# One written-out program order exchanged for another in a single-core RWKV-7 plus wave-mixer kernel

## The chip, the cores and the metric

One core of one Trainium2 chip. The metric is the device time of one launch in microseconds. Five engines work from queues of their own, each strictly in its program order: TensorE (PE), VectorE (DVE), ScalarE (ACT), GpSimd (POOL), and SyncE (SP), which here only issues transfers.

## The reference

The reference runs a state recurrence over 768 steps for 4 batches and 8 heads of width 40, and feeds its result, laid out as 4 x 768 x 320, to a mixer:

```python
for t in range(S):
    y[:, :, t] = np.einsum('bhd,bhde->bhe', rt, state)
    Sa = np.einsum('bhde,bhe->bhd', state, at)
    state_decay = state * wt[:, :, None, :] - np.einsum('bhd,bhe->bhde', Sa, bt)
    state = state_decay + np.einsum('bhd,bhe->bhde', vt, kt)
...
theta = x @ w_theta
zr, zi = x * np.cos(theta), x * np.sin(theta)
yr = np.einsum('ts,bsd->btd', w_tok_r, zr)
yi = np.einsum('ts,bsd->btd', w_tok_i, zi)
u = x + yr + yi
return u + np.maximum(u @ w_ch, 0.0)
```

## The kernel before

The 768 steps of a batch are cut into 6 chunks of 128; with 4 batches there are 24 chunks, numbered 0 to 23. The kernel first builds a list of 1610 operations (`plan.add`), each with an engine, a kind and a chunk number, and then emits them in an order that is written out by hand in the constant `ORDER`. Within an engine that order is the queue's order. `HOMES` gives the PSUM bank of each PSUM tile in the order in which they are opened, `PICK` lists the operations that take their second engine (a copy on DVE instead of ACT, a product on DVE instead of POOL, a mask on ACT followed by a select on POOL), and `WARM` puts dummy matmuls (L953) before a few early PE operations. No scheduler decides anything after that.

The names that the prediction uses, always with the chunk number behind them:

- SP loads (L408, L420): `lw`, `la`, `lk`, `lb`, `lv` bring one chunk of one input, 160 KB in pieces of 160 bytes; `loadr` brings half of a pair of chunks of `r` in pieces of 1280 bytes. Each load waits for the load eight places before it, and `st` stores a finished row block (L854).
- POOL: `kb` (L428, two of them per chunk, one from `lk` and one from `lb`) and `ah` (L428, from `la`) are products; `r` (L434) and `v` are casts; `wgt` (L650) is the new state; `z` (L811) are the mixer's products; `sel` (L568) is the select that completes a mask which was begun on ACT; `wdma` (L866, L894) starts a weight's transfer from POOL's queue.
- PE: `tkb`, `ta`, `tr` (L390, L524) are the transposes of `kb`, `ah`, `r`; `spsi`, `sphi`, `slv`, `slu` (L555) are score products, which use the array in two halves of 64 rows; `nu` (L614) needs the masked `phi` of its chunk; `gd` (L390) is the transpose of the state that `wgt` wrote; `wt` (L902) is the transpose of a mixer weight that `wdma` brought; `row` (L827) is the mixer's sum over tokens; `th` and `ch` (L711, L721) are the two dense products of the mixer.
- DVE: the four masks (L564, 1.2 us each), copies out of PSUM (L396) and small sums.

The recurrence runs from chunk to chunk; the loads and the preparation run one to four chunks ahead of it. The mixer's rows for one batch stand between the operations of the next batch, and those of the last batch at the end.

The emission itself is a plain loop:

```python
for o in plan.order():
    if o.idx in WARM:
        ...
    if o.fn is not None:
        o.fn()
```

Of the kernel before, what the change touches and what calls it, by code (L numbers as in the profile page):

```python
# [24 lines left out]
    0, 7, 3, 6, 1, 20, 2, 21, 23, 24, 32, 27, 8, 30, 22, 4, 33, 31, 9, 34, 25, 5, 26, 12, 28,  # L25
    11, 69, 35, 36, 10, 29, 70, 37, 47, 44, 40, 48, 72, 45, 38, 41, 18, 71, 49, 73, 39, 46, 98,
    19, 119, 99, 58, 14, 42, 100, 120, 57, 76, 15, 101, 122, 50, 121, 13, 123, 75, 74, 79, 106,
    102, 53, 107, 51, 131, 108, 16, 77, 125, 80, 52, 78, 109, 132, 126, 43, 81, 134, 124, 103,
    110, 133, 111, 82, 17, 84, 137, 104, 56, 138, 129, 112, 83, 85, 87, 130, 127, 54, 88, 156,
    128, 86, 59, 55, 157, 146, 89, 184, 143, 90, 147, 105, 158, 139, 60, 61, 159, 187, 97, 135,  # L30
    62, 164, 144, 188, 148, 160, 165, 96, 191, 140, 136, 161, 93, 166, 145, 141, 185, 167, 213,
    186, 194, 214, 149, 189, 142, 91, 162, 168, 150, 215, 163, 169, 190, 216, 92, 195, 221,
    234, 170, 151, 192, 152, 222, 246, 235, 193, 237, 217, 236, 95, 238, 202, 218, 94, 196,
    241, 203, 63, 197, 247, 155, 171, 239, 248, 219, 199, 172, 220, 198, 223, 249, 240, 200,
    271, 64, 267, 244, 272, 242, 299, 245, 205, 201, 273, 243, 224, 300, 173, 301, 154, 261,
    274, 254, 302, 174, 262, 225, 303, 279, 206, 175, 258, 306, 176, 255, 153, 259, 280, 263,
    250, 177, 204, 281, 256, 212, 275, 496, 282, 260, 211, 226, 251, 257, 305, 252, 320, 264,
    276, 253, 283, 317, 349, 227, 327, 265, 277, 328, 497, 304, 309, 278, 208, 329, 498, 284,
    310, 266, 499, 330, 207, 350, 285, 307, 351, 318, 286, 270, 308, 354, 331, 352, 500, 311,
    268, 332, 287, 361, 319, 314, 353, 312, 336, 269, 333, 539, 362, 337, 289, 356, 363, 209,  # L40
    315, 288, 313, 290, 364, 338, 355, 387, 210, 291, 339, 540, 292, 316, 365, 116, 388, 322,
    357, 366, 113, 541, 389, 359, 358, 340, 390, 501, 360, 367, 325, 334, 542, 503, 391, 368,
    382, 373, 392, 376, 412, 502, 374, 506, 369, 411, 504, 321, 377, 375, 393, 416, 507, 524,
    505, 370, 181, 394, 378, 525, 326, 508, 418, 335, 371, 526, 341, 372, 323, 415, 509, 395,
    396, 527, 413, 528, 342, 510, 514, 178, 511, 397, 517, 117, 529, 595, 545, 398, 512, 118,
    384, 530, 572, 399, 544, 532, 531, 573, 596, 515, 400, 513, 533, 574, 554, 597, 383, 401,
    543, 402, 417, 379, 575, 598, 516, 534, 385, 403, 380, 114, 599, 546, 581, 115, 548, 582,
    414, 535, 576, 381, 549, 550, 583, 404, 601, 555, 551, 577, 642, 536, 182, 324, 584, 557,
    578, 427, 179, 556, 567, 66, 558, 180, 183, 585, 561, 386, 428, 559, 537, 600, 586, 568,
    419, 602, 538, 560, 604, 587, 522, 429, 547, 605, 420, 606, 619, 421, 552, 607, 626, 562,  # L50
    553, 434, 423, 627, 564, 435, 422, 436, 565, 563, 643, 518, 628, 425, 437, 644, 610, 629,
    519, 566, 424, 613, 645, 603, 588, 611, 630, 520, 426, 589, 438, 698, 430, 635, 231, 646,
    523, 631, 612, 439, 636, 431, 632, 745, 440, 571, 608, 432, 614, 609, 699, 647, 521, 746,
    700, 675, 747, 648, 637, 570, 433, 615, 676, 616, 701, 633, 293, 677, 748, 651, 634, 678,
    638, 649, 590, 652, 684, 579, 569, 296, 685, 679, 617, 580, 639, 706, 653, 228, 591, 654,
    592, 657, 686, 680, 593, 618, 620, 661, 594, 687, 650, 441, 702, 711, 703, 621, 640, 442,
    712, 655, 662, 688, 681, 658, 656, 689, 705, 659, 622, 641, 682, 663, 660, 664, 690, 704,
    667, 749, 665, 691, 683, 709, 68, 692, 707, 710, 67, 729, 668, 666, 708, 694, 65, 693, 695,
    730, 750, 719, 697, 713, 720, 670, 696, 731, 232, 732, 294, 672, 233, 297, 714, 721, 295,
    733, 298, 738, 229, 751, 739, 734, 716, 715, 230, 740, 624, 717, 735, 754, 450, 752, 451,  # L60
    755, 778, 718, 452, 346, 625, 741, 779, 453, 881, 756, 343, 780, 623, 454, 757, 408, 781,
    882, 742, 764, 883, 405, 767, 765, 782, 884, 669, 673, 444, 783, 455, 443, 768, 456, 671,
    445, 766, 784, 446, 736, 885, 457, 785, 737, 458, 760, 743, 459, 753, 448, 786, 787, 887,
    722, 744, 796, 761, 788, 769, 758, 460, 763, 759, 789, 762, 461, 790, 462, 888, 797, 912,
    792, 463, 791, 447, 913, 793, 770, 795, 892, 771, 794, 914, 893, 723, 915, 772, 886, 674,
    802, 773, 890, 464, 803, 891, 347, 905, 465, 916, 348, 344, 799, 917, 805, 409, 345, 406,
    920, 804, 407, 896, 811, 726, 466, 921, 473, 897, 410, 474, 725, 808, 475, 918, 467, 809,
    724, 898, 468, 922, 469, 899, 927, 798, 449, 476, 471, 919, 477, 889, 906, 900, 801, 928,
    478, 929, 960, 470, 807, 480, 728, 930, 961, 901, 481, 482, 923, 806, 962, 955, 483, 963,
    894, 935, 484, 931, 479, 800, 969, 924, 895, 485, 970, 940, 983, 932, 486, 964, 727, 941,  # L70
    902, 965, 1030, 971, 934, 908, 903, 925, 972, 1031, 907, 819, 933, 820, 1032, 926, 904,
    487, 776, 810, 821, 1033, 488, 822, 984, 966, 775, 936, 985, 938, 1035, 937, 986, 823, 774,
    824, 939, 1086, 489, 825, 973, 490, 987, 777, 491, 1034, 949, 494, 946, 942, 812, 492, 813,
    950, 1087, 1037, 814, 1088, 1007, 974, 1036, 1089, 943, 951, 957, 975, 815, 990, 945, 816,
    947, 817, 493, 944, 1041, 989, 1039, 956, 1042, 818, 976, 948, 1040, 1014, 988, 958, 977,
    826, 1015, 952, 991, 827, 472, 1052, 953, 1090, 1016, 909, 967, 1017, 994, 992, 968, 995,
    1053, 979, 954, 993, 978, 1018, 1133, 996, 911, 1019, 1054, 980, 997, 998, 981, 1001, 1020,
    910, 999, 982, 828, 1023, 1002, 1092, 1058, 1134, 829, 1024, 959, 1000, 830, 1135, 1091,
    1004, 1049, 1005, 1136, 835, 1008, 1093, 836, 833, 1095, 831, 1009, 1063, 1003, 1050, 1096,
    837, 838, 1010, 1064, 1097, 1038, 1006, 1021, 1098, 1051, 1065, 1110, 1022, 1025, 1066,  # L80
    1104, 1026, 1045, 1043, 1072, 1044, 839, 1105, 840, 1067, 1073, 1027, 1011, 1046, 1068,
    1269, 1074, 841, 1047, 1069, 1012, 1270, 1075, 1028, 1048, 1094, 1013, 1271, 1117, 1138,
    1099, 1029, 1061, 1118, 1076, 1055, 1100, 1272, 1101, 1139, 1060, 1137, 1119, 1056, 1077,
    1120, 1059, 1140, 1070, 1126, 1071, 1142, 1102, 1057, 1127, 1161, 1106, 1144, 1143, 1121,
    1128, 1315, 1122, 1103, 1107, 1145, 1078, 865, 1123, 1108, 866, 1129, 867, 1111, 1141,
    1316, 1166, 1148, 1317, 1124, 1112, 1130, 1167, 1318, 1155, 1125, 1152, 1273, 1156, 1062,
    1146, 1168, 1276, 1149, 1169, 1113, 868, 1147, 1153, 1157, 869, 1275, 1150, 1131, 1115,
    1151, 1079, 1274, 1132, 1154, 870, 495, 1080, 1170, 1293, 871, 1280, 1319, 1109, 1278,
    1171, 1281, 1371, 1158, 1279, 1172, 1320, 1159, 1300, 1173, 1081, 1372, 1114, 1321, 1082,
    1301, 1083, 1373, 1284, 1294, 1174, 1277, 1084, 1287, 1374, 1085, 1302, 1322, 842, 1285,  # L90
    1116, 1303, 1324, 1160, 843, 1162, 844, 1325, 1286, 1304, 1295, 1308, 1305, 845, 1185, 846,
    1288, 1343, 1326, 1348, 1327, 847, 1187, 1309, 1163, 1334, 1349, 848, 1289, 1310, 1184,
    1335, 1350, 1175, 1351, 858, 1186, 859, 1311, 1336, 860, 832, 1352, 1188, 1164, 1357, 861,
    1353, 1411, 1312, 862, 1323, 1345, 1176, 863, 1330, 1191, 1313, 1358, 1412, 1296, 1314,
    1354, 1331, 1413, 864, 1337, 1376, 1333, 1165, 1414, 1359, 1282, 1332, 1338, 849, 1417,
    1283, 1328, 1395, 850, 1355, 1329, 1377, 1360, 1339, 852, 1396, 851, 1375, 1397, 1416,
    1415, 853, 1290, 1356, 1361, 856, 1340, 1398, 1378, 1177, 854, 1474, 1306, 1291, 1178,
    1404, 855, 1475, 1418, 1307, 1179, 1405, 1344, 1476, 1399, 1180, 1190, 1346, 1292, 1477,
# [45 lines left out]
WARM = {21: 25, 30: 4, 33: 1, 28: 8, 41: 11}  # L144
# [846 lines left out]
```

## Time and profile before

| what | value |
|---|---|
| time, median of 3 runs | 201.43 us (199.85 to 201.85) |
| profiled execution, first to last instruction | 203.2 us |
| busy PE, DVE, ACT, POOL | 191.8, 167.8, 150.7, 142.2 us |
| mean granted TensorE clock | 0.983 |
| input loads on SP | 144 |
| stores on SP | 24 |
| weight transfers on POOL | 18 |
| last matmul begins | 199.19 us |

The profiled execution is 1.8 us longer than the median of the unprofiled runs, and 1.4 us longer than the slowest of them. Busy times add up over the whole span; they say nothing of which engine another one waits for at a given place. A line of the timeline begins with the start in us and the duration in us, and ends, in brackets, with the idle time of the engine before it and what ended that idle time. SPq is the time that SP takes to issue a transfer, not the transfer itself.

### The profile page before, as it was taken

The page shows a single profiled execution, that of the slowest core. Times are in us where ns is not written, and L with a number is a line of the kernel's source. Part 1 is how long each engine was busy: PE and PEld are TensorE (multiplying, and loading weights), DVE is VectorE, ACT ScalarE, POOL GpSimd, SP SyncE. Part 2 cuts the span into 40 slices and gives each one's busy share as a digit, 9 for nine tenths or more (in the row PEclk, how much of TensorE's full clock was granted, in tenths as well). Part 3 has the DMA queues.
Part 4 walks back from the last instruction along what each step waited for, and adds up shares of the span by engine and source line. Part 5 has one row for each costly group of instructions (what it writes and reads, how often), then busy time and mean ns, then how long its engine had stood idle before and what let it go on. Part 6 is the DMA issues. An engine that isn't in the chain of part 4 may idle for free.

```text
span 203.2 us, 8123 instructions
## 1 busy us (share of the span) xinstructions
PE 191.8 (94%) x3354; PEld 155.5 (77%) x3354; DVE 167.8 (83%) x263; ACT 150.7 (74%) x345; POOL 142.2 (70%) x207
## 2 busy tenths in 40 slices
PE   7987999997699999999999999999999999999993
PEld 6775787985588788888878888888788878877761
DVE  5377899999489999889797988999999987768653
ACT  3585778899479988969988598888988976465210
POOL 8275655685788899889799949779499494319300
PEclk9999999999589999999999999999999999999999
DMA  6989899989698999999979899998985460110213
GB/s 119 205 163 194 162 181 193 202 155 197 123 198 150 176 176 195 189 215 219 170 166 192 160 213 164 182 162 171 187 167 102 97 166 0 35 59 10 100 65 129
DMA packets 127365, 31.03 MB, mean 153 GB/s; under 512 B 117664, under 2 KB 127328, under 8 KB 127328
## 3 DMA queue, kind: packets, MB, share of 16 engines
q1 hardware_dynamic: 124544, 27.54, 67.9%
q0 software_dynamic: 2784, 2.97, 9.4%
q8 instruction: 26, 0.43, 0.9%
q14 instruction: 11, 0.09, 0.1%
HBM read 29.54 MB, written 3.93 MB: 165 GB/s over the span
## 4 chain that ended last, share of the span: by engine, by line
PE 76%; SPq 7%; DMA 6%; DVE 4%; issue 2%; ACT 2%; POOL 2%; DVEq 0%; POOLq 0%; ACTq 0%
PE ps_s L827 17%; PE ps_s L390 13%; PE ps_d L555 10%; PE ps_s L711 7%; SPq L408 4%; PE ps_s L679 3%; DMA raw_r<-in_r_dram 3%; SPq L420 3%; PE ps_s L635 3%; PE ps_s L524 3%; PE ps_s L614 2%; PE ps_s L721 2%; DMA raw_a<-in_a_dram 2%; PE ps_s L750 2%; PE ps_s L748 2%
## 5 line engine op out<-in xcount | busy, mean ns | idle before, releaser
L428 POOL TENSOR_TENSOR kb<-raw_kb,ex 128x320 bf16<-128x320 f32 x46 | 36.8, 812 | 7.1 <-DMA raw_kb<-in_k_dram 2.9
L827 PE MATMUL ps_s<-zr,wtok_r 128*128 128x320 bf16 x132 | 37.5, 299 | 0.0
L827 PE MATMUL ps_s<-zi,wtok_i 128*128 128x320 bf16 x132 | 37.5, 299 | 0.0
L564 DVE TENSOR_TENSOR psi<-ps_d,mask_p 128x1024 bf16<-128x1024 f32 x22 | 26.8, 1217 | 4.0 <-PE ps_d L555 3.8
L564 DVE TENSOR_TENSOR lamu<-ps_d,mask_p 128x1024 bf16<-128x1024 f32 x23 | 27.8, 1214 | 0.3 <-PE ps_d L555 0.3
L564 DVE TENSOR_TENSOR phi<-ps_d,mask_n 128x1024 bf16<-128x1024 f32 x19 | 23.1, 1218 | 1.4 <-PE ps_d L555 1.4
L811 POOL TENSOR_TENSOR zi<-cs,xp 128x320 bf16<-128x320 f32 x21 | 16.4, 793 | 9.2 <-ACT cs L796 9.2
L564 DVE TENSOR_TENSOR lamv<-ps_d,mask_p 128x1024 bf16<-128x1024 f32 x17 | 20.7, 1218 | 2.6 <-PE ps_d L555 2.4
L428 POOL TENSOR_TENSOR ah<-raw_a,we 128x320 bf16<-128x320 f32 x22 | 19.0, 866 | 5.2 <-ACT we L470 2.4
L811 POOL TENSOR_TENSOR zr<-cs,xp 128x320 bf16<-128x320 f32 x21 | 16.6, 804 | 2.2 <-ACT cs L796 2.2
L650 POOL TENSOR_TENSOR gt<-sum,ex 128x320 bf16<-128x320 f32 x13 | 9.6, 737 | 11.5 <-DVE sum L646 8.4
L555 PE MATMUL ps_d<-aT,kbT 64*128 64x128 bf16 x384 | 17.3, 221 | 0.1
L827 PEld LDWEIGHTS <-wtok_r 128*128 128x128 bf16 x144 | 14.0, 97 | 4.1
L827 PEld LDWEIGHTS <-wtok_i 128*128 128x128 bf16 x144 | 14.0, 97 | 3.4
L390 PE MATMUL ps_s<-wide,kb 128*128 128x128 bf16 x192 | 15.3, 223 | 0.2
L748 PE MATMUL ps_s<-kb,lamv 128*128 128x40 bf16 x192 | 15.2, 183 | 0.0
L750 PE MATMUL ps_s<-kb,lamu 128*128 128x40 bf16 x192 | 15.1, 181 | 0.0
L555 PEld LDWEIGHTS <-kbT 64*128 64x128 bf16 x384 | 12.0, 96 | 3.4 <-issue 1.0
L434 POOL CAST r<-raw_r 128x640 bf16<-128x640 f32 x11 | 8.0, 723 | 8.8 <-DMA raw_r<-in_r_dram 8.8
L748 PEld LDWEIGHTS <-lamv 128*128 128x128 bf16 x192 | 13.7, 97 | 0.5
L851 DVE SCALAR_TENSOR_TENSOR oo<-ps_s,up 128x320 f32<-128x320 f32 x21 | 9.5, 485 | 5.0 <-PE ps_s L721 4.5
L750 PEld LDWEIGHTS <-lamu 128*128 128x128 bf16 x192 | 13.4, 99 | 0.1
(165 smaller groups left out, 616.1 us busy)
## 6 DMA issues: line engine op xcount, KB each, us to landing
raw_w<-in_w_dram SPq DMA_DIRECT2D x24, 160.0 KB, 4.4
raw_v<-in_v_dram SPq DMA_DIRECT2D x24, 160.0 KB, 4.0
raw_a<-in_a_dram SPq DMA_DIRECT2D x24, 160.0 KB, 3.8
raw_kb<-in_k_dram SPq DMA_DIRECT2D x24, 160.0 KB, 4.0
raw_kb<-in_b_dram SPq DMA_DIRECT2D x24, 160.0 KB, 3.9
raw_r<-in_r_dram SPq DMA_DIRECT2D x24, 160.0 KB, 3.9
out_dram<-oo SPq DMA_DIRECT2D x23, 160.0 KB, 2.1
wrow_i<-in_moe_w_tok_i_dram POOLq DMA_DIRECT2D x6, 192.0 KB, 5.2
```

The source lines that it names most:

```text
L390: nc.tensor.transpose(out=dst[:, c:c + 128], in_=pair(src, g), identity=ident)
L408: lambda dst=dst, src=src: nc.sync.dma_start(out=dst, in_=src),
L428: pool = ("POOL", lambda: nc.gpsimd.tensor_tensor(out=dst, in0=in0, in1=in1, op=ALU.mult))
L555: nc.tensor.matmul(t[:, q, g, :], lhsT=lhs[g][rows(q)], rhs=rhs[g][rows(q)], start=True, stop=True)
L564: add("DVE", kindm, i, lambda: nc.vector.tensor_tensor(out=flat, in0=whole(), in1=mask.to_broadcast([128, 2 * G, 128]), op=ALU.mult), 1217 ...
L650: add("POOL", "wgt", i, lambda: nc.gpsimd.tensor_tensor(out=new_state, in0=sum_t, in1=wm.to_broadcast([128, 8, D]), op=ALU.mult), 830, [(" ...
L711: nc.tensor.matmul(ps(pk)[:, 0:DM], lhsT=lhs[:, c * n + kt, :], rhs=wt[:, 3 * c + kt, :], start=kt == 0, stop=kt == 2, skip_group_check=n ...
L748: nc.tensor.matmul(o, lhsT=lamv[:, p, g, :], rhs=kb[:, 0, h, 0:D], start=first, stop=False, skip_group_check=True)
L750: nc.tensor.matmul(o, lhsT=lamu[:, p, g, :], rhs=kb[:, 1, h, 0:D], start=False, stop=True, skip_group_check=True)
L811: pool = ("POOL", lambda: nc.gpsimd.tensor_tensor(out=dst, in0=in0, in1=in1, op=ALU.mult))
L827: nc.tensor.matmul(acc(), lhsT=wtok[nm][j][:, s], rhs=zs[c][:, s], start=n == 0 and c == 0, stop=n == NT - 1 and c == 1)
L851: add("DVE", "oo", t, lambda ck=ck, u=u, oo=oo: nc.vector.scalar_tensor_tensor(out=oo, in0=ps(ck)[:, 0:DM], scalar=0.0, in1=u, op0=ALU.max ...
```

## The change

`ORDER`, `HOMES`, `PICK` and `WARM` are replaced; nothing else is. The same 1610 operations are there, with the same sizes and the same 144 loads, 24 stores and 18 weight transfers.

```diff
 ORDER = [
-    0, 7, 3, 6, 1, 20, 2, 21, 23, 24, 32, 27, 8, 30, 22, 4, 33, 31, 9, 34, 25, 5, 26, 12, 28,
...
+    3, 0, 6, 7, 1, 2, 20, 4, 23, 21, 8, 24, 27, 32, 5, 22, 33, 12, 30, 25, 35, 31, 10, 34, 38,
...
 HOMES = [
-    4, 5, 5, 6, 5, 4, 7, 0, 2, 5, 4, 6, 7, 4, 5, 2, 7, 4, 5, 0, 4, 7, 2, 4, 0, 5, 6, 7, 2, 5,
...
+    7, 5, 7, 6, 6, 7, 4, 2, 0, 5, 6, 7, 5, 0, 4, 5, 6, 7, 4, 7, 6, 2, 0, 6, 5, 7, 2, 4, 5, 0,
...
 PICK = [
-    25, 31, 37, 39, 40, 48, 49, 75, 80, 85, 86, 115, 118, 130, 172, 180, 193, 203, 204, 222,
...
+    25, 26, 27, 29, 31, 34, 35, 40, 75, 76, 78, 109, 110, 115, 118, 125, 126, 138, 147, 148,
...
-WARM = {21: 25, 30: 4, 33: 1, 28: 8, 41: 11}
+WARM = {23: 25, 33: 8, 38: 4, 44: 3}
```

Read as queues, the parts of the change that the prediction speaks of are these (places counted from 1 within the queue; operations between dots are in the queue's order).

| queue | before | after |
|---|---|---|
| SP, places 46 to 60 | lk7 lb7 loadr6 loadr6 lb8 loadr8 lw9 lk8 loadr8 la8 lw10 lb9 lk9 la9 lv8 | lk7 lb7 loadr6 loadr6 loadr8 lw9 la10 loadr8 lb8 lv8 loadr10 lk8 lw10 lb9 la8 |
| SP, place of lk8, la8, lb11, lk13, st0 | 53, 55, 73, 83, 85 | 57, 60, 74, 87, 91 |
| POOL around r6 | kb6 wdma2 wdma2 kb7 ah7 kb7 r6 z2 wdma3 z2 z2 z2 wdma3 kb8 kb8 | kb6 ah6 ah7 kb7 kb7 r6 wdma2 wdma3 wdma3 wdma2 z2 r8 z2 kb8 z2 kb8 |
| POOL, chunks 10 and 11 | wdma4 wgt8 kb10 kb10 wdma5 ah10 wdma5 wdma4 r10 v10 kb11 wgt9 | kb10 wgt8 ah10 kb10 kb11 v10 wdma4 wdma5 kb11 wdma4 wdma5 wgt9 |
| POOL, chunk 13 | wdma6 wdma6 wdma7 wdma7 sel10 sel12 r12 v12 kb13(b) sel12 ah13 kb13(k) z8 | wgt10 r12 wdma6 wdma6 wdma7 v13 kb13(k) z8 ah13 kb13(b) sel12 wdma7 |
| mixer products z on DVE | 4 | 12 |
| operations on POOL, DVE, ACT | 182, 238, 335 | 175, 246, 335 |
| changes of PE between 64-row and 128-row groups | 122 | 120 |
| dummy matmuls | 49 | 40 |

By the durations of the profile before, the engines' sums move little: DVE's planned operations from 176.9 to 181.8 us, POOL's from 143.7 to 137.5 us, ACT's from 161.9 to 163.1 us.

229 rows, old and new, of tables (HOMES, ORDER, PICK) are left out of this document.

## Prediction

> **What bounds the kernel now.** I read the page first, then the stages by windows, then the waits, then the timeline of the queues at the places where the stages change.
>
> ```profile
> PE 191.8 (94%) x3354; PEld 155.5 (77%) x3354; DVE 167.8 (83%) x263; ACT 150.7 (74%) x345; POOL 142.2 (70%) x207
> DMA  6989899989698999999979899998985460110213
> PE 76%; SPq 7%; DMA 6%; DVE 4%; issue 2%; ACT 2%; POOL 2%; DVEq 0%; POOLq 0%; ACTq 0%
> ```
>
> These lines of the page (busy times, DMA's row in 40 slices, the chain that ended last by engine) show two bounds, not one. PE carries 76% of the chain, but the DMA row stands at 8 or 9 tenths in nearly every slice up to about 158 us: for three quarters of the span the inputs come in as fast as the DMA engines bring them.
>
> ```profile
> 45.00:50.00 5.00, 4.38 (x85) 3.60 (x83) 4.93 (x8) 4.91 (x9) 3.61 (x6) 1.00 1.05 189
> 50.00:55.00 5.00, 2.24 (x36) 1.85 (x37) 2.10 (x3) 2.03 (x7) 3.00 (x5) 0.60 0.71 138
> 55.00:60.00 5.00, 5.00 (x105) 4.56 (x102) 4.21 (x6) 3.61 (x9) 4.81 (x7) 0.71 1.15 202
> 90.00:95.00 5.00, 5.00 (x100) 4.07 (x97) 4.22 (x8) 4.95 (x7) 5.00 (x8) 1.00 1.13 193
> ```
>
> By windows (PE, PE load, DVE, ACT, POOL busy, then granted clock, DMA share, GB/s) there is one hole: from 50 to 55 us PE works 2.24 us of 5, and its clock is granted at 0.60 and 0.71 up to 60. From 70 us on PE has next to no idle time.
>
> ```profile
> POOL r L434 <- DMA raw_r<-in_r_dram: 8.8, 4, 3.4
> PE ps_s L524 <- POOL r L434: 2.8, 1, 2.8
> ```
>
> ```profile
> 45.06 0.60 POOL L894 DMA_DIRECT2D wrow_i<-in_moe_w_tok_i_dram  x1
> 45.65 0.55 POOL L894 DMA_DIRECT2D wrow_r<-in_moe_w_tok_r_dram  x1
> 51.99 0.72 POOL L434 CAST r<-raw_r 128x640 bf16<-128x640 f32 x1 [3.37 <-DMA raw_r<-in_r_dram]
> 60.77 0.86 POOL L428 TENSOR_TENSOR ah<-raw_a,we 128x320 bf16<-128x320 f32 x1 [0.93 <-POOL zr L811]
> ```
>
> The waits and POOL's timeline name the hole: two weight transfers start at 45 us, the second half of `loadr6` lands only at 51.93 (6.9 us after its issue at 45.03; the median of such loads is 3.9), so `r6` and then `tr6` on PE come late, at 52.76.
>
> I also need PE's pace. I took the start-to-start step of every PE group from its timeline (a `row` pair 0.271 us, a 20-matmul `y` 0.546, a transpose of four 0.223, a score group 0.234 before another 64-row group and 0.318 before a 128-row one), the lower quartile for each kind. They add to 177.2 us before and 176.3 after, so the change removes no PE work to speak of: two mode changes fewer at 0.09 each, nine dummies fewer, both in a stage where PE waits anyway. What counts is when PE reaches an operation and how much PE work is left behind it. At `tr6` that is 142.35 us before and 141.71 after; at `ta8` 134.78 and 133.73; at `nu12` 100.86 and 100.89.
>
> **The change, part by part.**
>
> *The hole at 50 us.* After, no weight transfer stands ahead of `r6`; all four `wdma` of that stretch come behind it. The pair `loadr6` keeps SP's places 48 and 49. Without the two weights its second half should land about 1 us behind the load before it (48.18), 49.1, and `r6` with 0.72 ends near 49.8. `tr6` then starts at 49.9 instead of 52.76: 2.9 us gained. The slow clock behind the hole costs 2.0 us (the steps between 52.76 and 57.8 beyond their warm pace); without a hole it is gone too. PE then runs to `tkb8` and `ta8` 8.0 us of work later, at 57.9.
>
> *The next loads.* That gain has to be fed. `la8` goes from SP's 55th place to the 60th; `lb9`, `lv8`, `lw10`, `la10` and half of `loadr10` are put ahead of it, and the four weights run beside them. From the packet records a load of 160-byte pieces takes 0.95 us of all sixteen DMA engines, one of 1280-byte pieces 0.53 (the page has 67.9% of 203.2 us for 168 transfers, 0.82 on average). Lower end: `la8` landed at 58.28, plus 4 x 0.95 and 0.53 gives 62.6. Upper end: the load in the 60th place landed at 64.74. I take 63.6, the middle, since the queue is full there both times. `ah8` needs 0.15 and 0.87, so `ta8` starts at 64.7, against 62.42, with 1.05 us less work behind it: 1.2 us late. PE waits from about 57 to 61 for `tkb8` (`lk8`, 53rd to 57th place) and then for `ta8`, so the slow clock comes back here; most of it falls into the wait, 0.5 us does not. Together +1.7 us: the hole is moved, not removed.
>
> A rule bears on that clock. In the trace a hole of 2.8 us (`x06`'s last step ends at 49.98, `tr6` starts at 52.76) was enough for 0.60. The Trainium skill, page "TensorE: Matmul & The Clock Gate", Part 1, has the clock halved after an idle window of about 3.4 us, free-running. By that rule a wait of 1.7 us, such as the next one but one, costs nothing more; by the row of 2.8 us it is also below the shortest hole that has been seen to cost something. The sum therefore holds nothing for it, and the rival below holds 2.0.
>
> *Chunk 11.* `wgt9` now stands behind the `kb11` that needs `lb11` and behind two more weight issues. `lb11` landed at 78.13 and goes one place back: 78.1 to 80.8. Then 0.15, 0.82, 0.59, 0.54 and 0.74 make 81.0 to 83.6 for the end of `wgt9`, and `gd9` follows. PE, from 65.2 at `ta8`, is there 17.0 us later, at 82.2: a wait of 0 to 1.5, taken as 1.2. It moves PE only up to the next place.
>
> *Chunk 13.* This one decides.
>
> ```profile
> 93.80 0.84 POOL L428 TENSOR_TENSOR kb<-raw_kb,ex 128x320 bf16<-128x320 f32 x1
> 94.57 1.11 POOL L568 TENSOR_SCALAR_AFFINE_SELECT phi<-phi 128x1024 bf16<-128x1024 bf16 x1
> 95.63 0.87 POOL L428 TENSOR_TENSOR ah<-raw_a,we 128x320 bf16<-128x320 f32 x1
> 96.46 0.81 POOL L428 TENSOR_TENSOR kb<-raw_kb,ex 128x320 bf16<-128x320 f32 x1
> ```
>
> ```profile
> 97.49 0.36 PE L614 MATMUL ps_s<-nx,phi 128*128 128x40 bf16 x8
> ```
>
> Before, POOL does the `kb13` of `lb13`, then `sel12` (94.57), then the rest, and `nu12` starts on PE at 97.49. After, `sel12` stands behind the `kb13` of `lk13`, a `z8`, `ah13` and the other `kb13`; and `lk13` goes from SP's 83rd place to the 87th, with `lw14`, `lv13`, `lw16` and half of `loadr14` put ahead. Lower end: it landed at 91.78, plus 3 x 0.95 and 0.53 is 95.2. Upper end: the 87th load landed at 98.06, though SP stood idle before that,
>
> ```profile
> 88.28 0.59 SPq L408 DMA_DIRECT2D raw_w<-in_w_dram  x1
> 92.42 0.36 SPq L854 DMA_DIRECT2D out_dram<-oo  x1
> ```
>
> from 88.9 to 92.4, for the first store, which after comes four places behind `lk13`. I take the middle, 96.6. From there 0.15, then the steps of the rows above: 0.80, 0.76, 0.83, 0.77 and 1.09, so `sel12` ends at 101.0 and `nu12` starts at 101.1 (99.7 to 102.6). PE would be there at 65.2 + 32.8 + 1.2 = 99.2, so it waits 1.9 us. The work behind `nu12` is the same in both orders, so the shift is 101.1 - 97.49 = +3.6 us (2.2 to 5.1), which contains the earlier shifts. Queued behind that `sel12` on POOL are `wdma7` for the last `wt12` and eight `z8`/`z11`; they have 12.6 us of PE work until `ta14` and need 11.1, so nothing more is added.
>
> *The last batch.* Three more `z` go from POOL to DVE in the last 20 us. DVE ends `ex23` at 184.45 and then does `oo15` 0.48, a `z`, a copy 0.36, a `z`, two sums 0.90, and two `z`, before the third term of `row22`, which PE reaches, on the clock of before, at 188.5. A `z` on DVE took 1.03, 0.99 and 1.08 there, with POOL's products beside it, and 0.80 at 164 us; a DVE product of the same shape at the start took 0.50. With 1.03 the fourth ends at 190.3, 1.8 us late; with 0.50 at 188.2, not late. Some of POOL's products will lie beside them, some not: 0.80, which gives 0.9 us.
>
> *The rest.* In the first 20 us the loads set the pace in both orders (`la0` and `lw0` change places, the pair of `loadr0` lands 0.7 us earlier); whatever is gained there is waited for again at `ta8`: nothing. DVE's sum rises by 4.9 us and ACT's by 1.2, spread over stretches where PE is last: nothing is taken, and 0 to 1 us stays in the range.
>
> Sum, against the profiled 203.2 us: +3.6 and +0.9, 207.7 us. The unprofiled median is 201.43, so 205.9 us.
>
> **The rivals.**
>
> *The gain comes through (faster).* If the loads keep up, the hole at 50 us is worth its whole price: 2.9, the clock 2.0 and 0.6 of work done earlier, 5.5 us: 195.9. For it speaks SP's idle time before the first store: its 3.5 us are four loads at 0.82, as many as `lk13` is moved back, so the DMA engines are not the limit everywhere. It decides from `la8` at or before 57.5 and `lk13` before 93.4; against it stand five loads ahead of `la8` and a DMA share of 1.15 at 55 to 60. 0.22.
>
> *Only the wait at `ta8`.* If `lk13` lands before 93.4, `sel12` is done before PE arrives without the wait at chunk 11, and +1.7 is left: 203.1, a little more with DVE's products. 0.20.
>
> *Everything late.* `lk13` as the 87th load at 98.06 (+5.1), the clock dropping once more (2.0), and 0.9: 209.4. The DMA share of 1.13 in the window from 90 speaks for it; that SP no longer stops there, against. 0.11.
>
> *It does nothing.* The hole is exchanged for one of the same size at `ta8`, and POOL's order is covered by other waits: 201.4. 0.05.
>
> My forecast holds 0.42; its own range is 203.6 to 210.
>
> **How the numbers follow.** Within 1% (2.0 us) is about what a measurement of this kernel can tell from no change; the three runs shown lie 2.0 us apart. Faster by more takes the first rival, 0.22. Within 1% take the last rival and the larger part of the second, 0.20. Slower is the rest, 0.58. The range leaves out the lower half of the first rival's spread and the far end of the third: 196.5 to 210.0.
>
> **What would show it.** In the changed kernel's profile: `tr6` near 50 us and no wait of PE for `r` of 2.8 us; instead PE waiting for POOL's `ah` or `kb` of chunk 8 at 57 to 65 with a granted clock well under 1 there; PE's `nu` of chunk 12 waiting for `phi` from L569 near 101 us. I am wrong if PE is as free of idle time after 57 us as it was after 70 before, or if `la8` lands by 58 us.

## The result

The changed kernel takes 209.27 us (median of 4 runs, 208.20 to 211.28) against 201.64 us before (199.85 to 203.78): the ratio is 1.041, with an interval of 1.036 to 1.047. It is slower by 7.6 us; forecast were 4.5, with 209.27 still inside the range.

The page of the profiled execution (span 207.9 us), the same three lines that were shown of before:

```profile
PE 192.1 (92%) x3345; PEld 156.4 (75%) x3345; DVE 170.9 (82%) x271; ACT 152.3 (73%) x345; POOL 137.9 (66%) x200
...
DMA  6998999978998989999999997889972050013104
...
PE 60%; DMA 12%; DVE 7%; POOL 7%; ACT 6%; issue 4%; SPq 2%; POOLq 0%; DVEq 0%; ACTq 0%
```

PE is busy for as long as before (192.1 us against 191.8). What grew is the part of the chain that ends on PE that is not PE's: 40% instead of 24%, 12% of it DMA. Time was not added as work but as waiting. The stretch by windows (columns as above: PE, PE load, DVE, ACT, POOL busy, granted clock, DMA share, GB/s):

```profile
45.00:50.00 5.00, 4.78 (x103) 3.95 (x102) 4.86 (x8) 4.97 (x11) 5.00 (x8) 1.00 0.89 185
50.00:55.00 5.00, 4.57 (x106) 4.02 (x103) 5.00 (x8) 4.87 (x12) 3.08 (x5) 1.00 1.04 178
55.00:60.00 5.00, 2.55 (x46) 1.86 (x44) 3.82 (x4) 3.26 (x10) 1.82 (x3) 0.95 1.01 190
60.00:65.00 5.00, 4.22 (x44) 3.57 (x45) 2.01 (x3) 2.73 (x6) 5.00 (x8) 0.50 1.09 200
65.00:70.00 5.00, 5.00 (x104) 4.26 (x103) 4.18 (x8) 4.27 (x8) 4.99 (x8) 0.87 0.92 155
```

The hole that the profile of before has from 50 to 55 us is now at 55 to 60, and the clock of 0.50 follows behind it. PE's waits between 48 and 110 us (total, times, longest):

```profile
PE ps_s L391 <- POOL kb L429: 3.0, 1, 3.0
PE ps_s L615 <- POOL phi L569: 1.1, 1, 1.1
PE ps_s L903 <- DMA wrow_r<-in_moe_w_tok_r_dram: 0.9, 1, 0.9
PE ps_d L556 <- DVE lamv L565: 0.8, 1, 0.8
```

The largest is `tkb8` waiting for `kb8`. (The changed kernel's lines are one higher than those of before, and the experiments' differ by one or two.) POOL's timeline tells why, and also what happened at chunk 13:

```profile
47.97 0.71 POOL L435 CAST r<-raw_r 128x640 bf16<-128x640 f32 x1
48.63 1.12 POOL L895 DMA_DIRECT2D wrow_i<-in_moe_w_tok_i_dram  x2
49.74 1.08 POOL L895 DMA_DIRECT2D wrow_r<-in_moe_w_tok_r_dram  x2
...
58.14 0.80 POOL L429 TENSOR_TENSOR kb<-raw_kb,ex 128x320 bf16<-128x320 f32 x1 [3.50 <-DMA raw_kb<-in_b_dram]
...
59.73 0.80 POOL L429 TENSOR_TENSOR kb<-raw_kb,ex 128x320 bf16<-128x320 f32 x1
...
97.23 0.80 POOL L429 TENSOR_TENSOR kb<-raw_kb,ex 128x320 bf16<-128x320 f32 x1 [3.76 <-DMA raw_kb<-in_k_dram]
98.00 0.79 POOL L812 TENSOR_TENSOR zi<-cs,xp 128x320 bf16<-128x320 f32 x1
98.75 1.11 POOL L429 TENSOR_TENSOR ah<-raw_a,we 128x320 bf16<-128x320 f32 x1
99.82 0.80 POOL L429 TENSOR_TENSOR kb<-raw_kb,ex 128x320 bf16<-128x320 f32 x1
100.58 1.08 POOL L569 TENSOR_SCALAR_AFFINE_SELECT phi<-phi 128x1024 bf16<-128x1024 bf16 x1
```

`r6` is early, as forecast. Then four weight transfers are issued in a row, and the first `kb8` waits for `lb8`, which was issued at 49.27 and landed at 58.01. The second `kb8`, at 59.73, could not have come sooner either, since its `lk8` landed at 59.66. At chunk 13 the `kb13` of `lk13` waits until 97.23, and `sel12` ends at 101.66.

Landing times from the DMA records and start times on PE, in us. The last column is another profiled execution of the kernel before, from the first experiment, with a span of 201.9 us:

| | before | after | before, again |
|---|---|---|---|
| `loadr6`, second half, lands | 51.93 | 47.29 | 49.54 |
| `tr6` starts | 52.76 | 50.06 | 50.37 |
| `la8` lands | 58.28 | 62.19 | 57.37 |
| `ta8` starts | 62.42 | 64.06 | 58.45 |
| `gd9` starts | 80.72 | 83.44 | 77.54 |
| `lk13` lands | 91.78 | 97.09 | 91.55 |
| `nu12` starts | 97.49 | 101.72 | 96.26 |
| last matmul group starts | 199.19 | 203.86 | 197.97 |

Against the profiled execution of before, 4.7 us are lost, and `nu12` already has 4.2 of them.

### The profile page after: what moved, and what is told of

It is laid out like the page before. It is cut to its first block, busy times and chain, and to the rows that moved or that the text cites. A ratio compares the mean times of both kernels' runs of the same rounds, so it can differ in the third digit from the quotient of the medians.

```text
span 207.9 us, 8098 instructions
## 1 busy us (share of the span) xinstructions
PE 192.1 (92%) x3345; PEld 156.4 (75%) x3345; DVE 170.9 (82%) x271; ACT 152.3 (73%) x345; POOL 137.9 (66%) x200
## 4 chain that ended last, share of the span: by engine, by line
PE 60%; DMA 12%; DVE 7%; POOL 7%; ACT 6%; issue 4%; SPq 2%; POOLq 0%; DVEq 0%; ACTq 0%
PE ps_s L828 13%; PE ps_s L391 10%; PE ps_d L556 8%; PE ps_s L712 5%; DMA raw_kb<-in_b_dram 4%; DMA wrow_r<-in_moe_w_tok_r_dram 3%; DMA raw_kb<-in_k_dram 3%; PE ps_s L525 3%; PE ps_s L680 3%; POOL kb L429 2%; PE ps_s L636 2%; DVE zi L811 2%; POOL ah L429 2%; PE ps_s L615 2%; PE ps_s L751 2%
## 5 line engine op out<-in xcount | busy, mean ns | idle before, releaser
L429 POOL TENSOR_TENSOR kb<-raw_kb,ex 128x320 bf16<-128x320 f32 x44 | 35.5, 815 | 12.8 <-DMA raw_kb<-in_b_dram 4.4
L565 DVE TENSOR_TENSOR lamu<-ps_d,mask_p 128x1024 bf16<-128x1024 f32 x22 | 26.7, 1218 | 4.6 <-PE ps_d L556 4.3
L565 DVE TENSOR_TENSOR phi<-ps_d,mask_n 128x1024 bf16<-128x1024 f32 x20 | 24.3, 1216 | 0.4 <-PE ps_d L556 0.2
L565 DVE TENSOR_TENSOR lamv<-ps_d,mask_p 128x1024 bf16<-128x1024 f32 x19 | 23.1, 1216 | 1.7 <-PE ps_d L556 1.6
L565 DVE TENSOR_TENSOR psi<-ps_d,mask_p 128x1024 bf16<-128x1024 f32 x19 | 23.1, 1218 | 1.1 <-PE ps_d L556 0.9
L812 POOL TENSOR_TENSOR zi<-cs,xp 128x320 bf16<-128x320 f32 x17 | 13.9, 830 | 9.6 <-ACT cs L797 9.5
L812 POOL TENSOR_TENSOR zr<-cs,xp 128x320 bf16<-128x320 f32 x18 | 14.0, 794 | 4.5 <-ACT cs L797 4.0
L834 DVE TENSOR_TENSOR up<-ps_s,xp 128x320 bf16<-128x320 f32 x22 | 10.6, 485 | 6.3 <-PE ps_s L828 6.2
L391 PEld LDWEIGHTS <-kb 128*128 128x128 bf16 x192 | 12.3, 101 | 3.8 <-POOL kb L429 3.2
L619 ACT ACTIVATE nu<-ps_s 128x320 bf16<-128x320 f32 x24 | 10.7, 444 | 4.0 <-PE ps_s L615 4.0
```

Of the source, the lines that this page charges most:

```text
L391: nc.tensor.transpose(out=dst[:, c:c + 128], in_=pair(src, g), identity=ident)
L429: pool = ("POOL", lambda: nc.gpsimd.tensor_tensor(out=dst, in0=in0, in1=in1, op=ALU.mult))
L565: add("DVE", kindm, i, lambda: nc.vector.tensor_tensor(out=flat, in0=whole(), in1=mask.to_broadcast([128, 2 * G, 128]), op=ALU.mult), 1217 ...
L619: add("ACT", "enu", i, lambda: nc.scalar.mul(out=nu[:, :, 0:D], in_=ps(pk)[:, 0:DM].rearrange("p (h d) -> p h d", h=H), mul=-1.0), 437, [p ...
L812: pool = ("POOL", lambda: nc.gpsimd.tensor_tensor(out=dst, in0=in0, in1=in1, op=ALU.mult))
L834: add("DVE", "uadd", q, lambda: nc.vector.tensor_tensor(out=u, in0=acc(), in1=x, op=ALU.add), 488, [pk, x_key(q)], [u_key(q)], at="row")
```

## The experiments

Twelve kernels ran. A ratio is to the kernel before on the same chip. Four are the kernel before or an edit of it, eight are edits of the changed kernel. The stall of a stretch is the start-to-start steps of PE's groups minus their pace in the profile of before.

| edit | time, us | ratio (interval) |
|---|---|---|
| before, again | 201.26 | 0.996 (0.991 to 1.001) |
| before, two `wdma2` behind `r6` | 201.06 | 0.999 (0.994 to 1.005) |
| before, SP's queue of the changed kernel | 205.21 | 1.017 (1.009 to 1.025) |
| before, four weights in a row behind `r6` | 202.97 | 1.013 (1.005 to 1.021) |
| changed, SP's queue of before | 226.88 | 1.122 (1.112 to 1.133) |
| changed, loads of chunk 8 ahead | 210.79 | 1.047 (1.036 to 1.058) |
| changed, `sel12` behind the first `kb13` | 208.48 | 1.038 (1.027 to 1.049) |
| changed, weights spread | 206.79 | 1.025 (1.015 to 1.035) |
| changed, four edits | 212.77 | none: times 207.65 to 214.48 |
| changed, five edits | 207.43 | 1.032 (1.027 to 1.037) |
| changed, six edits | 206.77 | 1.030 (1.025 to 1.035) |
| changed, six edits and early loads put back | 205.42 | 1.025 (1.019 to 1.031) |

### Is the hole at 50 us part of every execution?

> The kernel before once more, unchanged. Theory 1: the hole at 50 us belongs to every execution of it; then the spans lie near 203 us, TensorE's mean granted clock near 0.98, and tr6 starts near 52.8 us. Theory 2: the profiled execution shown was a long one (all four executions of the changed kernel have a time 1.7 us above their span, so a time of 201.4 would go with a span of 199.7); then most spans lie near 200 us with a clock of 0.99 or more, and the hole is smaller or has a normal clock behind it.

This profile has a span of 201.9 us, a clock of 1.00 throughout, and no hole:

```profile
45.00:50.00 5.00, 3.79 (x74) 2.92 (x71) 4.96 (x9) 4.97 (x9) 3.41 (x6) 1.00 1.08 199
50.00:55.00 5.00, 4.63 (x120) 4.26 (x121) 4.54 (x7) 4.31 (x12) 4.96 (x8) 1.00 1.11 206
```

`tr6` starts at 50.37, with a wait of 1.0 us ahead of it instead of 2.8. Over 69 executions of this kernel, in this run and beside the others, the spans lie between 197.7 and 203.4 us with a median of 199.4, and every time is 1.65 to 1.77 us above its span. So the execution shown at the start, with 203.2, is at the long end. A mean granted clock as low as its 0.983 is found in one of the 69 only, and 65 of them have 0.99 or more: a hole with so long a slow clock is rare. Theory 2 holds. This second profile is itself the longest of its ten executions, so no profile shows one of the typical length.

```diff
-kb6 wdma2 wdma2 kb7 ah7 kb7 r6 z2
+kb6 kb7 ah7 kb7 r6 wdma2 wdma2 z2
```

> The kernel before with one edit: the two wdma2 stand behind r6 on POOL instead of ahead of kb7. Theory 1 (the two weights delay the second half of loadr6): it lands near 49 us instead of 51.9, tr6 starts at or before 50.5, and 2 to 4 us are gained against an execution with the hole. Rival (the loads of that stretch are late by themselves): the half lands after 51 us all the same and the time is that of before within 1 us.

The half landed at 47.88 and `tr6` started at 49.06. With the weights ahead of it the half had landed at 51.93 in one execution and at 49.54 in the other, so that one profile does not show how much of the gain is the weights'. The time does not change; the hole that this edit was to close is in few executions.

### The loads' order alone

```diff
 SP from place 46, kernel before with the changed kernel's loads and stores
-lk7 lb7 loadr6 loadr6 lb8 loadr8 lw9 lk8 loadr8 la8 lw10 lb9 lk9 la9 lv8 ...
+lk7 lb7 loadr6 loadr6 loadr8 lw9 la10 loadr8 lb8 lv8 loadr10 lk8 lw10 lb9 la8 ...
```

> The kernel before with SP's queue alone taken from the changed kernel (all 144 loads and 24 stores in its order); POOL, DVE, ACT, PE as before. Theory 1 (the loads' order makes the loss): lk8 and la8 land near 60 and 62 us, lk13 near 96, PE waits 2 to 4 us for chunk 8 and the time is 205 to 210. Rival (POOL's order and the engine variants make it): within 1.5 us of before.

`lk8`, `la8` and `lk13` landed at 57.51, 60.73 and 95.12, PE waited 2.3 us at `ta8`, and 1.7% is lost, at the lower edge of the first theory. That is less than half of the change's loss: there is no wait at `nu12`, because in POOL's order of before `sel12` does not stand behind `lk13`.

The reverse, the changed kernel with the first of these two lines instead of the second:

> The changed kernel with SP's queue alone taken from the kernel before. Theory 1 (the loads' order makes the loss): la8 lands by 58.5, lk13 by 92.5, the wait of PE at tkb8 goes from 3.2 us to under 1, and the time is 199 to 203. Rival (POOL's order and the engine variants): 206 to 209, with sel12 still late behind the kb13 of lk13.

Neither theory: 226.88 us. `la8` and `lk13` landed at 52.06 and 88.54, and yet `nu12` started at 104.31. SP's and POOL's timelines (SPq is the issue alone; it stands still from 85.2 to 95.4 before a store):

```profile
81.73 3.46 SPq L408 DMA_DIRECT2D raw_w<-in_w_dram  x1
95.36 0.36 SPq L854 DMA_DIRECT2D out_dram<-oo  x1
```

```profile
99.65 0.46 POOL L434 CAST v<-raw_v 128x320 bf16<-128x320 f32 x1 [8.58 <-DMA raw_v<-in_v_dram]
```

`st0` stands in SP's queue where `oo0` was ready in the order of before. Here PE makes it later, SP stops, the `lv13` behind the store is late, and POOL waits 8.6 us for it ahead of `kb13` and `sel12`. Over the whole run SP stood still for results of DVE's `oo` ten times, for 59.3 us. An in-order queue that waits for results can't be exchanged by itself, so this run says nothing on the loads.

### Chunk 8: the loads' places or the weights?

```diff
-loadr6 loadr6 loadr8 lw9 la10 loadr8 lb8 lv8 loadr10 lk8 lw10 lb9 la8
+loadr6 loadr6 lb8 lk8 la8 loadr8 lw9 la10 loadr8 lv8 loadr10 lw10 lb9
```

> The changed kernel with one edit on SP: lb8, lk8 and la8 go from places 54, 57 and 60 to 50, 51 and 52, ahead of loadr8, lw9, la10, lv8, loadr10, lw10, lb9. Both theories: the three land before 54 us, tkb8's wait of 3.2 us and the slow clock behind it vanish, and ta8 starts near 58.5 instead of 64.1. Theory 1 (as predicted: the place of lk13 sets nu12 by the clock on the wall): PE waits again for sel12, nu12 stays at 100 to 102 and the time at 207 to 209. Theory 2 (nu12 in the changed kernel only follows what was lost before; the mask that sel12 completes is itself ready only at 98.35, when PE has come that far): the gain is kept, nu12 comes at 96.5 to 98.5 and the time is 203.5 to 205.5.

The three landed before 50 us, and it gained nothing. The forecast that both theories shared fell:

```profile
PE ps_s L524 <- POOL r L434: 3.0, 1, 3.0
PE ps_s L390 <- POOL kb L428: 1.6, 1, 1.6
```

PE now waits for `r8`, since the second half of `loadr8` took the place of `lb8` behind the weights: issued at 49.4, landed at 58.5. No input landed between 53.2 and 58.0 us, as in the changed kernel (53.0 to 58.0).

```diff
-r6 wdma2 wdma3 wdma3 wdma2 z2 r8 z2 kb8 z2 kb8 z2 z2 v8 kb9 ah8
+r6 wdma2 z2 r8 wdma3 z2 kb8 wdma2 z2 kb8 wdma3 z2 z2 v8 kb9 ah8
```

> The changed kernel with one edit on POOL: of the four weight transfers that stand together behind r6, one stays, and the others go behind r8 and behind the two kb8; the loads keep their order. Theory 1 (the loads' places make chunk 8 late): lb8 lands at 56 to 58, tkb8 starts after 59.5, the time is 208 to 210. Theory 3 (the four weights in a row hold the loads issued beside them; lb8, issued at 49.3, took 8.7 us): lb8 lands by 55, tkb8 starts by 58, and 2 to 4 us are gained, 205 to 207.5.

Theory 3: `lb8` landed at 53.19, `tkb8` started at 58.00, no pause of the landings there is over 2.4 us, and 2.5 us are gained on the changed kernel; the two intervals of the ratio don't touch. A wait of 2.3 us for `ah8` stays. Of the single edits only this one is a clear gain. `lb8` alone would not prove the theory, as here it was issued at 48.84, ahead of the first weight (49.22). The loads issued beside the weights bear it out: `lk8` took 4.7 us from issue to landing. In the kernel of the next section where only `sel12` is moved, the four weights stand in a row; there `lb8`, issued 0.4 us ahead of them, landed at 53.31 too, but `lk8` took 8.0 us, and `tkb8` had to wait until 60.22.

```diff
 the kernel before
-kb6 wdma2 wdma2 kb7 ah7 kb7 r6 z2 wdma3 z2 z2 z2 wdma3 kb8 kb8
+kb6 kb7 ah7 kb7 r6 wdma2 wdma2 wdma3 wdma3 z2 z2 z2 z2 kb8 kb8
```

> The kernel before with one part of the change: all four weight transfers (wdma2, wdma2, wdma3, wdma3) stand in a row directly behind r6 on POOL; loads and everything else as before. Theory 3 (four weights in a row hold every load issued beside them for some 5 us): no input load lands for about 5 us around 53 to 58, kb8 or ah8 come late, PE waits 2 to 4 us at chunk 8 and the time is 203 to 206. Rival (the weights are harmless where they stand; only the loads' places count): within 1 us of before, 200.5 to 202.5.

The pause is there too: no input landed from 54.9 to 59.1 us. But in this profile PE does not pay for it (`ta8` at 58.84), as `lk8` and `la8` were issued before 50 us and landed at 51.35 and 54.92. The time is 1.3% longer, between what the two theories had; its four spans run from 199.8 to 202.7, and the profile is the shortest of them, so where the 1.3% lie isn't seen. What the traces show is that the weights in a row hold the loads issued beside them, and that PE waits when `lb8` or `lk8` is among these.

### Chunk 13, and several edits together

```diff
-kb13 z8 ah13 kb13 sel12
+kb13 sel12 z8 ah13 kb13
```

> The changed kernel with one edit on POOL: sel12 stands directly behind the first kb13 instead of behind that, a z8, ah13 and the other kb13. The mask begun on ACT is ready at 98.35 there, so sel12 ends near 99.5 instead of 101.7. Theory (sel12's place on POOL is the last wait at nu12): nu12 starts 1.0 to 1.3 us earlier and the time is 207.5 to 208.5. Rival (something else takes its place, ah13 or kb13 for ta13 and tkb13): no change, 208.5 to 210.

The wait of 1.2 us at `nu12` is gone and `nu12` starts at 100.03, but the run does not decide. In this execution `lk13` landed at 93.39 instead of 97.09, with no load moved: it was issued at 88.78, two us ahead of three weight transfers, and not 0.6 us ahead of them as in the changed kernel (90.73 and 91.33). POOL then waited for the mask:

```profile
97.92 1.10 POOL L568 TENSOR_SCALAR_AFFINE_SELECT phi<-phi 128x1024 bf16<-128x1024 bf16 x1 [3.59 <-ACT phi L566]
```

The `z8`, `ah13` and `kb13` would have fitted into those 3.6 us (they take 2.5), so `sel12` would have been as early without the edit. The interval of the time overlaps that of the changed kernel too. It does show that ACT's mask is the floor under `sel12`, and not `lk13` alone. ACT's own order makes that mask later than it need be:

```profile
91.27 1.03 ACT L566 ACTIVATE phi<-ps_d 128x1024 bf16<-128x1024 f32 x1
```

```profile
97.35 1.00 ACT L567 ACTIVATE phi<-ps_d 128x1024 bf16<-128x1024 f32 x1
```

The first line is of before, the second of the changed kernel. Before, the mask of chunk 12 stood ahead of the mixer's two sine operations in ACT's queue. In the changed kernel it stands behind them; they end at 97.44, while PE had its scores done by 95.55. No run moves it back.

```diff
 SP as in "loads of chunk 8 ahead", POOL's sel12 as above, and
-loadr12 loadr12 lw13 lv13 lb13 la13 lw16 lw14 lk13
+loadr12 loadr12 lw13 lk13 lv13 lb13 la13 lw16 lw14
-wdma4(i) wdma5(i) kb11 wdma4(r) wdma5(r) wgt9
+wdma5(r) wdma4(i) wdma5(i) kb11 wdma4(r) wgt9
```

> The changed kernel with four edits together: lb8, lk8, la8 ahead as in the first of these runs; lk13 six places ahead, before lv13; sel12 directly behind the first kb13; and the weight transfer that PE needs first of chunk 10's (the r half) issued first of its four instead of last. If the losses of the changed kernel sit at these places and add up (3.2 and 1.7 at chunk 8, 1.1 at the transpose of that weight, 1.2 at nu12), the time is 201 to 203; if a wait behind them takes over what is gained, 204 to 207.

The losses don't add up away: the four times scatter from 207.65 to 214.48, all above both ranges, and the profile is of the longest. With the loads of chunk 8 ahead PE waited 3.5 us for `r8` and 1.6 for `kb8`, and then 2.0 us for DVE, whose `z` took 3.61 us there:

```profile
73.17 3.61 DVE L810 TENSOR_TENSOR zi<-cs,xp 128x320 bf16<-128x320 f32 x1
```

```diff
 POOL as in "weights spread", sel12 and wdma5(r) as above, and
-loadr8 lb8 lv8 loadr10 lk8 lw10 lb9 la8
+loadr8 lb8 lk8 la8 lv8 loadr10 lw10 lb9
-DVE: mphi8 z5 mlv8        POOL: z5 r10
+DVE: mphi8 mlv8           POOL: z5 z5 r10
```

> The changed kernel with five edits: of the four weight transfers behind r6 one stays and the others go behind r8 and the two kb8; lk8 and la8 stand directly behind lb8 on SP (places 55 and 56); sel12 stands directly behind the first kb13; the r half of chunk 10's weight is issued first of its four; one z5 that took 1.82 us on DVE, ahead of the mask lamv of chunk 8, is on POOL again. If the waits of the changed kernel (3.2 and 0.6 at chunk 8 with 1.7 of slow clock behind them, 1.2 at sphi9, 1.1 at the first weight transpose of chunk 10, 1.2 at nu12) are its whole loss and are cured here without others in their place: 200.3 to 202.5. If something behind them takes over half of it: 203.5 to 206.

The time, 207.43, is above both ranges. The waits at `sphi9`, at the weight of chunk 10 and at `nu12` are gone, and that at `tkb8` is 0.5. In their place there is one of 3.7 us for `ah8`:

```profile
61.70 0.81 POOL L428 TENSOR_TENSOR kb<-raw_kb,ex 128x320 bf16<-128x320 f32 x1 [1.53 <-ACT gd L662]
62.46 0.86 POOL L428 TENSOR_TENSOR ah<-raw_a,we 128x320 bf16<-128x320 f32 x1
```

The page puts POOL's idle time down to ACT's `gd`, which was done by 61.53; the `lb9` that this `kb9` reads landed at 61.5. `la8` had landed at 56.2, six us before its `ah8` began: POOL's order makes chunk 8 wait for a load of chunk 9.

```diff
-kb8 wdma3 z2 z2 v8 kb9 ah8 z2 ah9 kb9
+kb8 ah8 wdma3 z2 z2 v8 kb9 z2 ah9 kb9
```

> The last kernel (the changed one with five edits) with a sixth on POOL: ah8 stands directly behind the second kb8 instead of behind kb9. There la8 had landed at 56.2, but ah8 stood behind the kb9 that waits for lb9 (landed 61.5) and ended only at 63.3, and PE waited 3.9 us for it. Theory (POOL's order turned the late lb9 into a wait for chunk 8): ah8 ends near 59, ta8 starts by 60, the wait and most of the 1.7 us of slow clock behind it go, and the time is 202 to 204. Rival (the loads cannot feed PE any faster there: what is gained at ta8 is waited for again at chunk 9): 205.5 to 207.5, with PE waiting for kb9 or ah9 near 63 to 67.

`ta8` starts at 59.20, as early as theory wanted, and the rival holds nonetheless:

```profile
PE ps_s L390 <- POOL kb L428: 2.4, 1, 2.4
PE ps_s L390 <- POOL ah L428: 0.9, 1, 0.9
```

The wait is now at `tkb9`, for the `kb9` of `lk9`, which landed at 63.40.

```diff
-lw9 la10 loadr8 lb8 lk8 la8 lv8 loadr10 lw10 lb9 la9 lk9 loadr10 lv10 lk11 lv9 lk10 lw12
+lw9 loadr8 lb8 lk8 la8 lv8 lw10 lb9 lk9 la9 loadr10 loadr10 lv10 lk11 lv9 lk10 la10 lw12
-la13 lw16 lw14 lk13
+la13 lk13 lw16 lw14
```

> The last kernel (the changed one with six edits) with SP's early loads put back: la10 and the first half of loadr10, which are needed only by chunk 10, go from places 52 and 58 to 67 and 61, lk9 ahead of la9 (place 59 instead of 62), and lk13 goes from 87 to 85. In the last kernel lk9 landed at 63.4 and PE waited 2.5 us for its kb9, and 1.6 us at chunk 13. Theory 1 (what is left is loads brought out of the order of need): lk9 lands by 61.5, the wait at tkb9 falls below 1 us, nu12 comes 1.5 to 3 us earlier (94.5 to 96), and the time is 203 to 205. Rival (the rate of the loads is the limit whatever their order): the wait goes on to chunk 10, nu12 stays near 97.4 and the time at 206 to 207.5.

`lk9` landed at 59.79, and the time is 205.42, within 0.5 us of theory 1's upper end. But `tkb9` still waited 1.6 us, two waits of 1.5 and 0.75 us followed at chunk 10, and `nu12` stayed at 97.31 as the rival had it. The median fell by 1.3 us, but the two intervals of the ratio (1.025 to 1.035 and 1.019 to 1.031) overlap, so a gain in time is not shown. The trace shows the load earlier, and part of what it could bring waited for again.

By the ratios the change lost 4.1%, and the edits together give 1.6 of it back. Of the 2.5% that stay the cause is open: the waits at chunks 9 and 10 are the large ones in the trace, and of the operations that `PICK` puts on other engines only one was put back. No version of the changed kernel beats the kernel before.

## Why the prediction was right, and where it was not

**The hole at 50 us.** `tr6` was forecast at 49.9 and came at 50.06; the half of `loadr6` at 49.1 and 47.29. The step was right against the execution shown, but its price of 2.9 and 2.0 us is not in the second profile of before, where `tr6` starts at 50.37 at full clock, and by the clocks of the 69 executions it is in few.

**Chunk 8.** Forecast: the hole is moved, `la8` at 63.6, `ta8` at 64.7, clock low again. Measured: 62.19, 64.06, and 0.50. The size was about right (`la8` just under the lower bound of 62.6) and the cause half right. The five loads ahead of `la8` were named, the four weights only as running beside them; it is their standing in a row that held `lb8` for 8.7 us and `lk8` until 59.66, and spreading them won 2.5 us. `ah8` then began 0.95 us after `la8` had landed, behind a `kb9` on POOL, which the prediction did not see either.

**The clock.** Of the slow clock behind this wait 0.5 us was to show. By their pace, PE's steps between `ta8` and `spsi8` lose 0.9, those between `tkb8` and `ta8` some 1.2, hidden behind `ah8`, which ended only at 64.0. The sum held nothing for waits under 2.8 us. The waits of 1.1 to 1.2 us left the clock at 1.00, as did one of 1.5 in before, again; but behind the 2.4 us for `kb9` in the six-edit kernel it was granted at 0.92 and 0.74 in the two windows of 5 us from 60, and behind a wait of 1.8 us for `kb8`, which ended at 60.22 in the kernel with `sel12` moved, at 0.59 and 0.73. The Trainium skill, page "TensorE: Matmul & The Clock Gate", Part 1, has an idle window of about 3.4 us; the traces agree on the waits up to 1.5 us, and show a reduced clock behind 1.8 and 2.4 us already. So the wait of 1.7 us (1.9 in its sum) that the prediction let pass for nothing could have cost something; that the one at `nu12` was shorter is luck.

**Chunk 11.** `gd9` was forecast at 83.4 after a wait of 1.2 us, and came at 83.44 after a wait of that size (1.24 us beyond PE's pace). The equal size is chance, for the place was wrong: it was not `wgt9` behind late loads, but `sphi9`, whose bank the mask `lamv` had not yet read, because a `z` moved to DVE stood ahead of it and took 1.82 us. "DVE's sum rises by 4.9 us and ACT's by 1.2 [...] nothing is taken" is the step that failed here.

```profile
69.81 1.82 DVE L811 TENSOR_TENSOR zi<-cs,xp 128x320 bf16<-128x320 f32 x1
71.55 1.21 DVE L565 TENSOR_TENSOR lamv<-ps_d,mask_p 128x1024 bf16<-128x1024 f32 x1
```

**Chunk 13.** Forecast: `lk13` at 96.6, `sel12` done at 101.0, `nu12` at 101.1, PE waiting 1.9 us. Measured: 97.09, 101.66, 101.72 and 1.2. PE came later than reckoned, since the weight that PE's order wants first for chunk 10 is issued last of its four: 1.1 us that the prediction did not see. And `lk13` was not the only thing behind `sel12`: the mask that it completes was ready on ACT only at 98.35, in part because ACT's order had changed too (see the run with `sel12` moved); the prediction looked at SP's and POOL's alone. Nor does the place in SP's queue fix when `lk13` lands. In the seven kernels that have it 87th it landed between 91.31 and 97.09, and in before, 83rd, at 91.78. In the changed kernel SP stood still ahead of `lw14`, the load just before it:

```profile
SPq L409 <- ACT lw L445: 3.9, 1, 3.9
```

`lk13` was issued only at 90.73 and then took 6.4 us beside three weight transfers. A sum of loads times 0.95 us has neither, so that 96.6 came so near is in part luck. The shift there, +4.2 us against +3.6 forecast, is right to 0.6.

**The last batch.** 0.9 us was taken; from `gd22` (+4.2) to the end (+4.7) it is 0.4. The `z` on DVE took 0.48 to 0.84 us there, not 1.03.

**From the profile to the time.** Here the miss in the time lies. The sum of 207.7 for the profiled execution met 207.9. Then 1.8 us were taken off, "the unprofiled median is 201.43, so 205.9". But a time is 1.7 us above its span in all executions, so a span can't be set beside times as the table of before does; the time that belongs to the span of 203.2 is 204.9, 3.5 us above the median, and the sum gives 209.4, against 209.27 measured; the forecast of 205.9 is 3.4 us too low. The median of before belonged to executions of some 199.7 us, few of them with the hole. The hole should have been priced as an event of some executions: then nothing of it is gained, and the loss is that much larger.

**The rivals.** That the gain comes through: no; the hole was closed, but few executions had it. Only the wait at `ta8`: no, `nu12` follows. Everything late: its 209.4 is the number that came out, though not by its sum; `lk13` was late by 5.3 us, but the clock did not fall a second time.

## What to carry to other kernels

Before a stall in a profile is priced, ask whether its execution is typical: compare its span, plus the fixed distance between span and time, with the median. When the transfers are the pace, look at what is issued beside a burst of weights, and whether an in-order queue puts a product of a late load ahead of one whose load is there. A wait that is cured by moving one load comes back at the load that gave way: read the next two waits before counting the gain. Where one order is exchanged for another, compare every engine's queue: here ACT's had a part in it, and the prediction did not look at it.

## What the runs showed of the hardware

Four weight transfers of 192 KB, issued on POOL's queue within 2.2 us, stand in six of the kernels. The loads that SP issued between the first and the last of them took 6.5 to 9.2 us from issue to landing, but for one of 5.0; with the weights spread, in four kernels, loads issued among them took 3.8 to 6.8. No load landed for 4.1 to 5.8 us in five of the six, and for 2.9 in the one with `sel12` moved; spread, the longest such pause was 2.4 to 3.2. In the changed kernel five loads landed within 2.2 us right after it (58.0 to 60.2).

The loads did not stand still meanwhile. From 54 to 56 us in the changed kernel, SP's queue has 310 packet records, mostly of 160 bytes and with a median of 27 ns, and moved 49 KB; POOL's has 235, mostly of 1536 bytes and with a median of 134 ns, and moved 333 KB. From 56 to 58, with 34 records of POOL left, SP's queue moved 464 KB. The Trainium skill, page "DMA: Bandwidth & Descriptors", Queues, rings and completion order, has each DMA engine take turns between the queues that have work, a packet at a time; records of both queues in like numbers, with the long ones taking most of the time, fit that.

A product of two SBUF tensors on DVE, 0.48 us by itself, took 0.8 to 1.4 us in many places and 1.63, 1.82 and 3.61 us in three kernels; POOL's products and casts ran beside these three for 0.9 to all of their time. POOL's own products of this kind took 0.78 to 1.10 us. In the longest case POOL's products lasted until 76.4 and DVE's ended at 76.78. The Trainium skill, page "SBUF — State Buffer", Who interferes with whom, states that such an instruction contends with a POOL instruction that reads SBUF and that the later one is blocked until the earlier one ends; the trace shows it kept back through several POOL instructions, not one.
